# Spectral filter and expert kernel: six filter steps of the first pair exchanged by DMA, the filter in 128 rows, products of the identity ahead of stage 2

## The chip, the cores and the metric

The kernel runs on one core of a Trainium2 chip. The metric is the device time of one execution in microseconds. Three runs of the kernel before gave 2653.4, 2653.47 and 2656.06, median 2653.47. One execution was profiled.

## What is computed

Three layers follow each other on 24,576 rows of 256 float32 values (8 sequences of 3,072):

```python
def _attn_ref(x, filt_r, filt_i):             # x: (8, 3072, 256)
    X = np.fft.rfft(x, axis=1)
    return np.fft.irfft(X * (filt_r + 1j * filt_i)[None], n=x.shape[1], axis=1)

def _moe_ref(x, w_in, w_out, g_ln):           # dense layer, 1024 wide
    h = x @ w_in
    solu = h * softmax(h)
    return (layernorm(solu) * g_ln) @ w_out

def _moe2_ref(x, expert_emb, tau, w1, w2):    # 8 experts, each row goes to one
    e = argmax(normalized(x) @ normalized(expert_emb).T / tau)
    return gate * (np.maximum(x @ w1[e], 0.0) @ w2[e])
```

## The kernel before

**Filter layer.** Two sequences make a complex pair, so there are four pairs, 0 to 3. A transform of 3,072 points is split into 64 by 48. For each pair `fft` runs three stages. Stage 1 (`stage1`, 12 chunks) makes transforms of 64 on TensorE and writes them to bufA in DRAM. Stages 2 and 3 run in one loop over 16 steps j of four columns each: load the step's rows from bufA (`load2`, two DMAs in the first pair, L577), multiply with the 48-point transform (stage 2, L657), apply the filter on VectorE (`filt`), multiply with the inverse 48-point transform (stage 3, L688 to L694), evict (L695) and write to bufC in DRAM (L701). In an iteration j of the loop stand the filter of step j-1, stage 2 of step j and stage 3 of step j-2. A last transform of 64 is made in `inv4`, together with the dense layer.

The filter needs a row and its mirrored row (real with imaginary part). The first pair has it in one way, the others in another. In the first pair stage 2 stays in PSUM (tile h, two buffers, freed by the last filter product), VectorE makes two products from it (L599 with the imaginary, L600 with the real part of the filter, in zw), and stage 3 takes both with two matrices, one of them with the mirroring in it: L688 and L694. In the other pairs stage 2 is evicted by ScalarE to z in SBUF, two DMAs on SP exchange its halves of 48 rows (L669, L670, `zw<-z`), VectorE makes three products (L603, L609, L611) and stage 3 has one. These pairs run beside the dense layer; the first pair runs alone, beside the preparation of the weights (`prep_b`), of which one unit is put out after each yield of `fft`.

The filter's values for two steps (ft, 96 rows, 10 KB a row) are loaded by `load_f` on SP into one of two buffers. In the first pair load_f(0) stands behind load2(0) and load2(1).

A float32 product is two records on TensorE; a step's stage 2 is two products of 512 columns (four records), its stage 3 in the first pair four products (eight records). Each queue and each engine works in the order in which its instructions are written; SP's loads therefore wait behind an earlier load that cannot be issued yet. DMAs issued by SP and ScalarE count on one of eight semaphores, and a DMA whose semaphore is still in use waits at issue.

**Dense layer** (`stage_b`): 192 tiles of 128 rows. For a tile j the matrix product with w_out (L994) ends in a PSUM tile o; ScalarE squares it (L1002), VectorE copies eight routing columns (raw, L1019), and one iteration later `half` scales the row to two float16 parts (ScalarE L1024, VectorE L1025) and a DMA writes them to xs. After the last tile `early` is drained (tables and loads of the first expert blocks).

**Expert layer** (`stage_c`): for each block of 256 rows of one expert VectorE copies its weights (L1215, two parts), TensorE makes the first product (L1259), then the second (L1226). It starts with `weights(0, 0)`, then `next(side)`, which resumes `stage_b` at its end, then `weights(0, 1)`.

Of the kernel before, what the change touches and what calls it, by code (L numbers as in the profile page):

```python
# [24 lines left out]
E = 8  # L25
# [12 lines left out]
SPLIT = 38  # L38
WAIT = 4
SPARE = 2  # L40
TURNED = ((34, 42), (28, 42), (24, 46))
MAGIC = 0x5F3759DF

# [48 lines left out]
def layout(inputs):  # L92
    k = np.arange(KF)[None, :] + N1 * np.arange(N2)[:, None]
    k = np.minimum(k, S - k)
    f = np.stack([inputs["filt_r"][k], inputs["filt_i"][k]], axis=2)
    f = np.stack([f, f], axis=0).reshape(2 * N2, KF, 2, D)
    d = {
        "x": inputs["x"],
        "filt": f,
        "w_in": inputs["moe_w_in"],  # L100
        "w_out": inputs["moe_w_out"],
        "g_ln": np.asarray(inputs["moe_g_ln"]).reshape(8, 128).T,
        "emb": inputs["moe2_expert_emb"],
        "tau": np.asarray(inputs["moe2_tau"], dtype=np.float32).reshape(1, 1),
        "w1": inputs["moe2_w1"],
        "w2": inputs["moe2_w2"],
    }
    for n in ("w_in", "w_out"):
        if d[n].dtype == np.float64:
            d[n] = np.ascontiguousarray(d[n]).view(np.int64)  # L110
    d.update(constants())
    return {n: np.ascontiguousarray(a) for n, a in d.items()}
# [40 lines left out]
class Build:  # L153
# [390 lines left out]
    def fft(self, p, ap, ps, hp):  # L544
# [12 lines left out]
        av = bufA.rearrange("c n k d -> (c n) k d") if p else bufA.rearrange("c k n d -> c n k d")  # L557
        ld, fts, halves, zs, ys = {}, {}, {}, {}, {}

        def first(j):  # L560

            return j // 2 * KC + j % 2 * (N1 // 2)

        def load_f(j):
            if j % 2 == 0 and j < n:
                ft = ap.tile([96, KC + 1, 2, D], F32, name="ft", tag="ft")
                nc.sync.dma_start(ft, a["filt"][:, first(j):first(j) + KC + 1, :, :])
                fts[j // 2] = ft

# [22 lines left out]
        def filt(j):  # L592

            m = j % 2
            z, zw, y = zs.pop(j)
            ft = fts[j // 2]
            fr, fi = ft[:, m:m + KC, 0, :], ft[:, m:m + KC, 1, :]
            if p == 0:
                nc.vector.tensor_tensor(y, z, fi, op=ALU.mult)  # L599
                nc.vector.tensor_tensor(zw, z, fr, op=ALU.mult)  # L600
                ys[j] = (y, zw)
                return
            nc.vector.tensor_tensor(y, z, fr, op=ALU.mult)  # L603
            yield
            k = 0
            if j == 0:
                nc.vector.scalar_tensor_tensor(zw[:, 0:1, :], zw[:, 0:1, :], self.sg0, fi[:, 0:1, :], op0=ALU.mult, op1=ALU.mult)
                k = 1
            nc.vector.scalar_tensor_tensor(zw[:, k:, :], zw[:, k:, :], self.sg[m], fi[:, k:, :], op0=ALU.mult, op1=ALU.mult)  # L609
            yield  # L610
            nc.vector.tensor_tensor(y, y, zw, op=ALU.add)  # L611
            ys[j] = (y,)

        if p > 0:
            load_f(0)
            yield
            self.flush()
            yield
            yield
        load2(0)  # L620
        load2(1)
        if p > 0:
            yield
            load2(2)
            yield
            yield
            split(0)
            load2(3)
            yield
            yield  # L630
            split(1)
        else:
            load_f(0)
            load2(2)
            load_f(2)
            split(0)
        for j in range(n + 2):
            steps = filt(j - 1) if 1 <= j <= n else iter(())
            next(steps, 0)
            if j < n:  # L640
# [3 lines left out]
                a2 = halves.pop(j)  # L644
                if p == 0:
                    w = hp.tile([128, KC, D], F32, name="h", tag="h")
                    z = w[:96]
                else:
                    z = ap.tile([96, KC, D], F32, name="z", tag="z", bufs=2)
                for i in range(0, KC, b):  # L650
# [4 lines left out]
                        nc.scalar.activation(z[:, i:i + b, :], t[:96], AF.Copy)  # L655
                    else:
                        nc.tensor.matmul(w[:96, i:i + b, :], self.d2f[m], a2[:, i:i + b, :])  # L657
                    if i == 0:
                        self.flush()
                        load2(j + (4 if p > 0 else 3))  # L660
# [4 lines left out]
                    yield  # L665
                    next(steps, 0)
                zw = ap.tile([96, KC, D], F32, name="zw", tag="zw")
                if p > 0:
                    nc.sync.dma_start(zw[0:48], z[48:96])  # L669
                    nc.sync.dma_start(zw[48:96], z[0:48])  # L670
                y = ap.tile([96, KC, D], F32, name="y", tag="y", bufs=3)
# [10 lines left out]
            if j >= 2:  # L682
# [2 lines left out]
                co = ap.tile([128, KC, D], F32, name="out", tag="out", bufs=3)[:96]  # L685
                for i in range(0, KC, b):
                    t = ps.tile([128, b, D], F32, name="a", tag="a")
                    nc.tensor.matmul(t[:96], self.d3[m], y[-1][:, i:i + b, :], start=True, stop=p > 0)  # L688
                    if p == 0:
                        k = 0  # L690
                        if i == 0 and j == 2:
                            nc.tensor.matmul(t[:96, 0, :], self.d3s[0], y[0][:, 0, :], start=False, stop=False)
# [203 lines left out]
    def stage_b(self, xp, bps, gp, ps, hp, op, aux, early):  # L896
# [76 lines left out]
        for i in range(n + LAG):  # L973
# [7 lines left out]
                nc.scalar.activation(L["s"], L["h"], AF.Exp, bias=L["nm"], scale=self.isc_h[:, i // N2:i // N2 + 1], accum_out=col(i, "st", 0))  # L981
            if now:
                nc.vector.scalar_tensor_tensor(L["s"], L["h"], col(i, "cc", 0), L["s"], op0=ALU.mult, op1=ALU.mult, accum_out=col(i, "st", 1))  # L983
            if half:
                half()
                half = None
            self.catch_up()
            if 0 <= j < n:
                T = live.pop(j)["T"]
# [26 lines left out]
            if puts:  # L1016
                puts.pop()()
            if 0 <= j < n:
                nc.vector.tensor_copy(g["raw"][:, k, :], o[:, D:D + E])  # L1019
                finals = [(f, next(f) if x == 3 else x) for f, x in finals]  # L1020

                def half(j=j, k=k, o=o, c2=c2, rows=rows):
# [18 lines left out]
        for _ in early:  # L1041
            pass
        yield
        if half:
            half()
            puts.pop()()
        while finals:
            yield
            finals = [(f, x) for f, x in ((f, over(f, next(f, 1))) for f, _ in finals) if x != 1]
# [379 lines left out]
```

## Time and profile before

| | us |
|---|---|
| median of three runs | 2653.47 |
| profiled execution, whole | 2659.22 |
| its span, first to last instruction | 2657.40 |
| stage 1 of the first pair | 0 to 48.6 |
| stages 2 and 3 of the first pair | 52 to 162 |
| dense layer with the other pairs | 162 to 1600 |
| expert layer | 1603 to 2657 |

In the span TensorE is busy 2586.2 us (97%), VectorE 1864.6 (70%), ScalarE 1511.8 (57%), GpSimd 1390.7 (52%). Names in the rows: PE is TensorE's products, PEld its weight loads, DVE VectorE, ACT ScalarE, POOL GpSimd, SP SyncE; a q behind a name is that engine's queue, where DMAs are issued. Each row names the line of the kernel. PEclk is TensorE's granted clock as a share of 2.4 GHz: 0.50 is 1.2 GHz.

### The profile page before, as it was taken

Reading aid. Unit: us, or ns where it says so; the run is one execution under the profiler, and the core shown is the slowest. Engines: PE = TensorE matmul, PEld = TensorE weight load, DVE = VectorE, ACT = ScalarE, POOL = GpSimd, SP = SyncE. Lnnn points to the kernel's source line nnn. Section 1 sums busy time; section 2 is a strip of 40 time slices with the busy share of each in tenths; the row PEclk is TensorE's granted clock in tenths of the full one; section 3 lists DMA queues with packets and bytes.
Section 4 is the critical chain, followed back from the end, with each engine's and each line's share of the span. In section 5 each row is a group of like instructions: output and inputs, shape, how many; then the busy total and the mean of one; then the engine's idle time right before and its main releaser. Section 6 shows DMA issues by size and latency. Waiting matters only on the chain.

```text
span 2657.4 us, 53169 instructions
## 1 busy us (share of the span) xinstructions
PE 2586.2 (97%) x19720; PEld 1974.9 (74%) x19720; DVE 1864.6 (70%) x2955; ACT 1511.8 (57%) x2836; POOL 1390.7 (52%) x2631
## 2 busy tenths in 40 slices
PE   5989999999999999999999999999999999999998
PEld 3447666676666776666777768888888888888897
DVE  1846999869999679998899875555545545445465
ACT  2357888777888777888788862323333333333332
POOL 1001456545677445676645657655555555555444
PEclk8999999999999999999999999999999999999999
DMA  9989989999999999998655533322332222332222
GB/s 311 234 264 241 225 205 198 238 251 203 207 216 210 278 217 201 191 215 164 133 130 129 109 75 77 82 75 76 77 76 76 77 75 77 76 76 76 75 58 56
DMA packets 494997, 400.62 MB, mean 151 GB/s; under 512 B 347435, under 2 KB 417205, under 8 KB 491664
## 3 DMA queue, kind: packets, MB, share of 16 engines
q1 hardware_dynamic: 460272, 331.53, 55.3%
q0 software_dynamic: 26704, 56.16, 7.2%
q10 hardware_dynamic: 7760, 9.51, 1.2%
q8 instruction: 156, 2.56, 0.4%
q14 instruction: 105, 0.86, 0.1%
HBM read 196.46 MB, written 103.09 MB: 113 GB/s over the span
## 4 chain that ended last, share of the span: by engine, by line
PE 44%; POOL 21%; issue 20%; DVE 8%; DMA 4%; ACT 2%; POOLq 0%; SPq 0%; ACTq 0%; DVEq 0%
PE h L765 14%; PE o L994 14%; POOL crow L1181 9%; POOL out_dram L165 7%; POOL scr L164 3%; PE a L688 3%; PE h L942 3%; PE a L747 2%; PE a L514 2%; PE a L654 1%; DVE nm L931 1%; DVE es L983 1%; DMA in<-in_x_dram 1%; DVE hl L960 1%; PE o L1226 1%
## 5 line engine op out<-in xcount | busy, mean ns | idle before, releaser
L994 PE MATMUL o<-wo_h,T 128*128 128x264 f16 x3072 | 549.8, 276 | 0.3 <-issue 0.2
L1226 PE MATMUL o<-cw,chh 128*128 128x256 f16 x3152 | 522.2, 273 | 0.4 <-issue 0.4
L994 PEld LDWEIGHTS <-T 128*128 128x128 f16 x4608 | 449.9, 98 | 90.1 <-issue 22.9
L1259 PEld LDWEIGHTS <-cw 128*128 128x128 f16 x5184 | 471.2, 98 | 56.2 <-issue 6.5
L765 PE MATMUL h<-win_h,xh 128*128 128x512 f16 x1536 | 491.2, 381 | 1.8 <-ACT xh L752 0.8
L934 POOL TENSOR_SCALAR gcc<-nm 128x1 f32<-128x1 f32 x192 | 164.4, 856 | 527.2 <-DVE nm L932 527.0
L1263 DVE SCALAR_TENSOR_TENSOR chl<-h,chh 128x512 f16<-128x512 f32 x197 | 134.5, 683 | 433.1 <-ACT chh L1262 405.6
L1226 PE MATMUL o<-cw,chl 128*128 128x256 f16 x1576 | 429.6, 273 | 0.0
L765 PEld LDWEIGHTS <-xh 128*128 128x128 f16 x2304 | 221.6, 98 | 278.7 <-issue 45.9
L994 PE MATMUL o<-wo_l,T 128*128 128x264 f16 x1536 | 423.8, 276 | 0.0
L165 POOL DMA_INDIRECT out_dram<-cot,ids x197 | 213.4, 1083 | 394.4 <-ACT cot L1229 384.7
L1226 PEld LDWEIGHTS <-chh 128*128 128x128 f16 x3152 | 307.5, 98 | 35.6 <-issue 0.2
L1229 ACT ACTIVATE cot<-o,fac 128x256 f32<-128x256 f32 x197 | 93.2, 474 | 411.2 <-PE o L1226 403.5
L1215 DVE COPY cw<-wexp 128x4096 f16 x216 | 289.4, 1347 | 38.3 <-PE o L1226 25.6
L931 DVE TENSOR_REDUCE nm<-h 128x1 f32<-128x1024 f32 x192 | 234.2, 1220 | 115.1 <-PE h L765 113.5
L1259 PE MATMUL h<-cxT,cw 128*128 128x256 f16 (+1 forms) x2592 | 291.9, 264 | 4.5 <-DVE cw L1215 4.1
L1259 PE MATMUL a<-cxT,cw 128*128 128x256 f16 (+1 forms) x2592 | 291.5, 263 | 1.6 <-issue 0.8
L765 PE MATMUL h<-win_l,xh 128*128 128x512 f16 x768 | 292.1, 380 | 0.0
L1181 POOL DMA_INDIRECT crow<-xs,ids x197 | 247.5, 1256 | 63.1 <-issue 63.1
L983 DVE SCALAR_TENSOR_TENSOR es<-h,gcc,es 128x1024 f32<-128x1024 f32 x192 | 243.9, 1270 | 18.8 <-ACT es L981 8.6
L981 ACT ACTIVATE es<-h,nm,isc_h 128x1024 f32<-128x1024 f32 x192 | 230.5, 1201 | 40.0 <-DVE nm L932 39.5
L165 POOL DMA_INDIRECT lst<-gdi,gix x192 | 208.9, 1088 | 36.5 <-issue 34.3
(255 smaller groups left out, 4272.1 us busy)
## 6 DMA issues: line engine op xcount, KB each, us to landing
wst<-in_w_dram SPq DMA_DIRECT2D x128, 256.0 KB
ft<-in_filt_dram SPq DMA_DIRECT2D x32, 960.0 KB
in<-in_x_dram SPq DMA_DIRECT2D x48, 512.0 KB
c<-bufC SPq DMA_DIRECT2D x96, 256.0 KB
xs<-rows SPq DMA_DIRECT2D x96, 256.0 KB
bufA<-out SPq DMA_DIRECT2D x72, 256.0 KB
in<-bufA SPq DMA_DIRECT2D x48, 384.0 KB
zw<-z SPq DMA_DIRECT2D x96, 192.0 KB
```

Source lines behind the costliest of these rows:

```text
L165: ins = self.nc.gpsimd.indirect_dma_start(in_offset=None, **kw).ins
L765: nc.tensor.matmul(h[:, nb, :], l[:, i, db, :], r[:, db, sl], start=k == 0, stop=k == 5)
L931: nc.vector.tensor_reduce(x[:, 0:1], L["h"], axis=AX.X, op=ALU.max, negate=True)
L934: nc.gpsimd.tensor_scalar(cc, nm, nm, 1.0, op0=ALU.mult, op1=ALU.max)
L981: nc.scalar.activation(L["s"], L["h"], AF.Exp, bias=L["nm"], scale=self.isc_h[:, i // N2:i // N2 + 1], accum_out=col(i, "st", 0))
L983: nc.vector.scalar_tensor_tensor(L["s"], L["h"], col(i, "cc", 0), L["s"], op0=ALU.mult, op1=ALU.mult, accum_out=col(i, "st", 1))
L994: nc.tensor.matmul(o[:, :D + E], T[:, l, :], r[:, f, :], start=q == 0, stop=q == 23)
L1181: nc.gpsimd.indirect_dma_start(out=rows[:, h, :], out_offset=None, in_=self.xs, in_offset=bass.IndirectOffsetOnAxis(ap=tab["ids"][:, h, k: ...
L1215: nc.vector.tensor_copy(w.rearrange("p (o k) -> p o k", o=1), self.wexp[:, bass.ds(e, 1), part * 4096:(part + 1) * 4096])
L1226: nc.tensor.matmul(o[:, :D], l[f // fs][:, f % fs, h * 128:(h + 1) * 128], w2[:, r, f, :], start=q == 0, stop=q == 23)
L1259: nc.tensor.matmul(t[:, i, :], w1[:, l, db, f * 128:(f + 1) * 128], xT[:, r + db, :n], start=q == 0, stop=q == 5)
L1263: nc.vector.scalar_tensor_tensor(hl[-1][:, sl, :], t, 0.0, hh[-1][:, sl, :], op0=ALU.max, op1=ALU.subtract)
```

## The change

- `SWAPPED` names six odd steps (3 to 13) of the first pair that go the way of the other pairs: ScalarE evicts stage 2 to z (two copies, z has two buffers), SP exchanges the halves with two DMAs, VectorE makes three products, stage 3 has one product a half instead of two. `twice(j)` tells whether a step has two products.
- The filter array has 128 rows instead of 96 (zeros below), in all four pairs; VectorE reads the first 96.
- load_f(0) of the first pair stands ahead of everything else behind stage 1. Behind it stand 18 products of the 128 x 128 identity with itself into a PSUM tile that nobody reads.
- At the end of `stage_b` half of tile 190, raw of tile 191 and half of tile 191 are written behind `early` and the first yield, so in the program behind `weights(0, 0)` of the expert layer.

```diff
--- before.py
+++ after.py
@@ -38,6 +38,8 @@
 SPLIT = 38
 WAIT = 4
 SPARE = 2
+WARM = 18
+SWAPPED = (3, 5, 7, 9, 11, 13)
 TURNED = ((34, 42), (28, 42), (24, 46))
 MAGIC = 0x5F3759DF
 
@@ -94,6 +96,7 @@
     k = np.minimum(k, S - k)
     f = np.stack([inputs["filt_r"][k], inputs["filt_i"][k]], axis=2)
     f = np.stack([f, f], axis=0).reshape(2 * N2, KF, 2, D)
+    f = np.concatenate([f, np.zeros((128 - 2 * N2, KF, 2, D), f.dtype)])
     d = {
         "x": inputs["x"],
         "filt": f,
@@ -557,13 +560,17 @@
         av = bufA.rearrange("c n k d -> (c n) k d") if p else bufA.rearrange("c k n d -> c n k d")
         ld, fts, halves, zs, ys = {}, {}, {}, {}, {}
 
+        def twice(j):
+
+            return p == 0 and j not in SWAPPED
+
         def first(j):
 
             return j // 2 * KC + j % 2 * (N1 // 2)
 
         def load_f(j):
             if j % 2 == 0 and j < n:
-                ft = ap.tile([96, KC + 1, 2, D], F32, name="ft", tag="ft")
+                ft = ap.tile([128, KC + 1, 2, D], F32, name="ft", tag="ft")
                 nc.sync.dma_start(ft, a["filt"][:, first(j):first(j) + KC + 1, :, :])
                 fts[j // 2] = ft
 
@@ -594,8 +601,8 @@
             m = j % 2
             z, zw, y = zs.pop(j)
             ft = fts[j // 2]
-            fr, fi = ft[:, m:m + KC, 0, :], ft[:, m:m + KC, 1, :]
-            if p == 0:
+            fr, fi = ft[:96, m:m + KC, 0, :], ft[:96, m:m + KC, 1, :]
+            if twice(j):
                 nc.vector.tensor_tensor(y, z, fi, op=ALU.mult)
                 nc.vector.tensor_tensor(zw, z, fr, op=ALU.mult)
                 ys[j] = (y, zw)
@@ -611,8 +618,12 @@
             nc.vector.tensor_tensor(y, y, zw, op=ALU.add)
             ys[j] = (y,)
 
+        load_f(0)
+        if p == 0:
+            t = ps.tile([128, 512], F32, name="a", tag="a")
+            for _ in range(WARM):
+                nc.tensor.matmul(t[:, :128], self.ident, self.ident)
         if p > 0:
-            load_f(0)
             yield
             self.flush()
             yield
@@ -630,7 +641,6 @@
             yield
             split(1)
         else:
-            load_f(0)
             load2(2)
             load_f(2)
             split(0)
@@ -644,7 +654,7 @@
                 a2 = halves.pop(j)
                 if p == 0:
                     w = hp.tile([128, KC, D], F32, name="h", tag="h")
-                    z = w[:96]
+                    z = w[:96] if twice(j) else ap.tile([96, KC, D], F32, name="z", tag="z", bufs=2)
                 else:
                     z = ap.tile([96, KC, D], F32, name="z", tag="z", bufs=2)
                 for i in range(0, KC, b):
@@ -655,6 +665,8 @@
                         nc.scalar.activation(z[:, i:i + b, :], t[:96], AF.Copy)
                     else:
                         nc.tensor.matmul(w[:96, i:i + b, :], self.d2f[m], a2[:, i:i + b, :])
+                        if not twice(j):
+                            nc.scalar.activation(z[:, i:i + b, :], w[:96, i:i + b, :], AF.Copy)
                     if i == 0:
                         self.flush()
                         load2(j + (4 if p > 0 else 3))
@@ -665,7 +677,7 @@
                     yield
                     next(steps, 0)
                 zw = ap.tile([96, KC, D], F32, name="zw", tag="zw")
-                if p > 0:
+                if not twice(j):
                     nc.sync.dma_start(zw[0:48], z[48:96])
                     nc.sync.dma_start(zw[48:96], z[0:48])
                 y = ap.tile([96, KC, D], F32, name="y", tag="y", bufs=3)
@@ -685,8 +697,8 @@
                 co = ap.tile([128, KC, D], F32, name="out", tag="out", bufs=3)[:96]
                 for i in range(0, KC, b):
                     t = ps.tile([128, b, D], F32, name="a", tag="a")
-                    nc.tensor.matmul(t[:96], self.d3[m], y[-1][:, i:i + b, :], start=True, stop=p > 0)
-                    if p == 0:
+                    nc.tensor.matmul(t[:96], self.d3[m], y[-1][:, i:i + b, :], start=True, stop=not twice(j - 2))
+                    if twice(j - 2):
                         k = 0
                         if i == 0 and j == 2:
                             nc.tensor.matmul(t[:96, 0, :], self.d3s[0], y[0][:, 0, :], start=False, stop=False)
@@ -981,9 +993,10 @@
                 nc.scalar.activation(L["s"], L["h"], AF.Exp, bias=L["nm"], scale=self.isc_h[:, i // N2:i // N2 + 1], accum_out=col(i, "st", 0))
             if now:
                 nc.vector.scalar_tensor_tensor(L["s"], L["h"], col(i, "cc", 0), L["s"], op0=ALU.mult, op1=ALU.mult, accum_out=col(i, "st", 1))
-            if half:
+            if half and j < n - 1:
                 half()
                 half = None
+            tail, half = [half], None
             self.catch_up()
             if 0 <= j < n:
                 T = live.pop(j)["T"]
@@ -1016,7 +1029,9 @@
             if puts:
                 puts.pop()()
             if 0 <= j < n:
-                nc.vector.tensor_copy(g["raw"][:, k, :], o[:, D:D + E])
+                raw = lambda g=g, k=k, o=o: nc.vector.tensor_copy(g["raw"][:, k, :], o[:, D:D + E])
+                if j < n - 1:
+                    raw()
                 finals = [(f, next(f) if x == 3 else x) for f, x in finals]
 
                 def half(j=j, k=k, o=o, c2=c2, rows=rows):
@@ -1041,9 +1056,9 @@
         for _ in early:
             pass
         yield
-        if half:
-            half()
-            puts.pop()()
+        for f in (tail[0], raw, half):
+            f()
+        puts.pop()()
         while finals:
             yield
             finals = [(f, x) for f, x in ((f, over(f, next(f, 1))) for f, _ in finals) if x != 1]
```

## Rows read from the trace of the kernel before

**Rows 1.** Windows: busy us of each engine (instructions), PEclk, DMA share, GB/s.

```profile
20.00:30.00 10.00, 5.74 (x24) 4.31 (x24) 0.00 (x0) 2.99 (x5) 1.50 (x3) 1.00 1.03 415
...
60.00:70.00 10.00, 8.89 (x23) 5.13 (x22) 4.10 (x5) 0.78 (x2) 0.00 (x0) 0.50 1.04 186
...
65.86:148.97 83.11, 81.06 (x228) 35.56 (x227) 71.01 (x109) 35.83 (x67) 0.00 (x0) 0.95 0.98 247
```
**Rows 2.** Timeline, stage 2's start: start, us, engine, line, operation [idle before <-releaser].

```profile
47.61 1.03 PE L514 MATMUL a<-in,wst 128*128 128x256 f32 x4
...
52.34 2.10 SPq L577 DMA_DIRECT2D in<-bufA  x4
54.49 0.43 SPq L567 DMA_DIRECT2D ft<-in_filt_dram  x1
...
56.74 3.70 PE L657 MATMUL h<-in,cst 96*96 96x512 f32 x4 [8.10 <-issue]
...
65.86 1.22 DVE L599 TENSOR_TENSOR y<-h,ft 96x1024 f32<-96x1024 f32 x1 [15.88 <-DMA ft<-in_filt_dram]
67.00 1.21 DVE L600 TENSOR_TENSOR zw<-h,ft 96x1024 f32<-96x1024 f32 x1
...
68.32 3.70 PE L657 MATMUL h<-in,cst 96*96 96x512 f32 x4 [1.11 <-DVE zw L600]
```
**Rows 3.** Timeline: y of steps 2, 14, 15; last eviction of stage 3.

```profile
74.95 1.21 DVE L599 TENSOR_TENSOR y<-h,ft 96x1024 f32<-96x1024 f32 x1
...
148.97 1.21 DVE L599 TENSOR_TENSOR y<-h,ft 96x1024 f32<-96x1024 f32 x1
...
152.57 1.22 DVE L599 TENSOR_TENSOR y<-h,ft 96x1024 f32<-96x1024 f32 x1
...
161.95 0.59 ACT L695 ACTIVATE out<-a 96x512 f32<-96x512 f32 x1 [0.33 <-PE a L694]
```
**Rows 4.** Chain that ended last, in order: start us, us, what, records.

```profile
149.90 1.72 PE h L657 x4
151.62 0.86 PE a L688 x2
...
207.35 0.89 PE a L747 x8
```
**Rows 5.** Lines L609, L611, pairs 1 to 3: ns min/median/max, first, last start.

```profile
L609 DVE SCALAR_TENSOR_TENSOR zw<-zw,cst,ft x48: 1007/1274/1282, 281.9 to 1219.2; 96x1024 f32<-96x1024 f32 x45, 96x768 f32<-96x768 f32 x3
L611 DVE TENSOR_TENSOR y<-y,zw x48: 1205/1214/1240, 286.9 to 1220.6; 96x1024 f32<-96x1024 f32 x48
```
**Rows 6.** Waits of VectorE, 65 to 149 us: us in total, times, longest.

```profile
DVE es L294 <- DMA T<-in_w_in_dram: 5.0, 1, 5.0
DVE wo_l L408 <- ACT wo_h L405: 3.4, 2, 2.0
```
**Rows 7.** Waits of SP's queue, 65 to 149 us.

```profile
SPq L577 <- DMA bufC<-out: 25.4, 5, 7.7
```
**Rows 8.** Timeline: first products of TensorE after two gaps.

```profile
28.19 1.97 PE L514 MATMUL a<-in,wst 128*128 128x256 f32 x8 [3.24 <-DMA wst<-in_m_dram]
...
192.42 2.07 PE L514 MATMUL a<-in,mt 128*128 128x256 f32 x4 [3.83 <-ACT out L515]
```
**Rows 9.** Timeline where the expert stage begins.

```profile
1600.54 0.17 DVE L1019 COPY graw<-o 128x8 f32<-128x8 f32 x1 [4.70 <-ACT rows L1002]
...
1601.91 1.47 DVE L1215 COPY cw<-wexp 128x4096 f16 x1
...
1603.49 2.55 PE L1259 MATMUL h<-cxT,cw 128*128 128x256 f16 x12 [4.05 <-DVE cw L1215]
...
1605.83 2.11 PE L1259 MATMUL a<-cxT,cw 128*128 128x256 f16 x12
...
1607.77 1.47 PE L1259 MATMUL h<-cxT,cw 128*128 128x256 f16 x12
```
**Rows 10.** Windows, columns as in rows 1: 100 us under the other pairs.

```profile
500.00:600.00 100.00, 99.30 (x669) 74.25 (x668) 67.02 (x129) 70.66 (x135) 41.96 (x123) 1.00 1.01 259
```

## The prediction

> **What bounds the kernel now.** I read the windows first, to see which engine is full in the stages that the diff touches, then the timeline where stage 2 of the first pair starts, then who waits for whom there, and last the timeline where the expert stage begins. Between these two places TensorE is busy 99% of a typical 100 us [rows 10], so a microsecond won in either should arrive whole at the end.
>
> Stage 1 ends at 47.61 + 1.03 = 48.6 us. Its rows go out to DRAM and come back, and the first product of stage 2 starts at 56.74, at half speed: four records span 3.70 us, where they later take 1.72 [rows 2, 4]. The clock stays at 0.50 from 60 to 70 [rows 1]. VectorE cannot start its first filter product until 65.86: it stood 15.88 us, and what came last was the filter, ft, queued on SP behind four loads that need stage 1's rows [rows 2]. From that product to the one of step 14 (65.86 to 148.97, 83.11 us) TensorE is busy 81.06 us, VectorE 71.01, and the DMA engines 0.98 of the time, at 247 GB/s [rows 1, 3]. One engine is full, but two others stand close behind it, and that decides what the swap is worth.
>
> **The change, part by part.** The sum is made against the profiled span of 2657.40 (2659.22 with what lies around it). The median of the three runs is 2653.47, 5.75 lower; I take the same differences off it.
>
> *Start of stage 2.* load_f(0) no longer stands behind loads that wait for bufA and can issue while SP idles before 52.34 [rows 2]. The 15.88 us wait goes, and step 0's product is late next. The 18 products are 36 records of 128 columns. Eight such take 0.89 us [rows 4], so 36 take 4.0: from 48.6 to 52.6. They lie in idle time and cost nothing unless the first load lands before that, and at 52.34 it is only being issued. They leave a gap of 52.6 to 56.7, 4.1 us. The nearest rows: after 3.24 us of idle, eight records of 256 columns still took 1.97 us, but after 3.83 us four took 2.07 [rows 8]. The gap is nearer to the second, so I take half speed for the start of stage 2, and full speed as the other bound. At half speed TensorE goes as in the trace up to h(2), which there waited 1.11 us for zw(0) [rows 2]; without that it starts at 67.2 and ends 3.70 later, so y(2) starts at 70.9 against 74.95 [rows 3]: **4.0 us won**. At full speed VectorE's own chain decides, with its first product at 56.74 + 1.72 = 58.5: 7.3 us.
>
> *Six exchanged steps.* On TensorE each loses the L688 product in both halves, two times 0.86 us [rows 4], 10.3 us in all. But VectorE gets three products from SBUF instead of two from PSUM, two of 1.21 us and one of 1.27 [rows 5]; two follow each other 1.14 apart (65.86 and 67.00), so a step costs about 1.25 more, 7.5 in all. ScalarE gets two copies a step of 0.59 us each, like an eviction of the same size [rows 3], 7 us in all, under 47 us of idle (busy 35.83 of 83.11 [rows 1]); without that cover each would make the exchange 0.6 us later. So from y(0) to y(14) VectorE's work goes from 71.0 to 78.5, and TensorE's falls to about 68.5 (81.1, less 8.6 for five swapped steps whose stage 3 lies inside, less 4 for the part at half speed). VectorE becomes the engine that paces. Its idle in the stretch, 12.1 us now, then counts in full: 5.0 for one T load, 3.4 for ScalarE, the rest in small waits [rows 1, 6]. ScalarE's stay. The T loads have no ft(0) in front of them any more and should come earlier by about as much as VectorE does. I take 7.5 us of idle, with bounds of 4 and 12. The stretch becomes 78.5 + 7.5 = 86.0 instead of 83.1: **2.9 lost**. After y(14) TensorE had a backlog: 13.0 us to the last eviction at 161.95. With VectorE pacing there is none: 3.6 us to y(15), 2.35 for its two products and four times 0.86 on TensorE, 9.4 in all [rows 3, 4]: **3.6 won**.
>
> The new wait is VectorE's on the exchange. Its second product of a swapped step blocks all that stands behind it in order: the preparation's conversions, the next filter product, and through that TensorE's h of a later step. SP issues the two DMAs behind in(j+3) and ft, and behind any wait of these; SP already spends 25.4 us there on bufC stores before it can issue a load [rows 7]. A step's rows are ready some 8 us after VectorE finished step j-3 (h, four products, h, a copy) and wanted 13 to 19 us after it, so 5 to 11 us are free for the transfer. I count nothing beyond the 7.5; the bad bound is the third rival.
>
> *Filter in 128 rows.* By bytes each of the 32 loads grows by a third. With loads of 128 rows the engines moved 415 GB/s at a share of 1.03, with loads of 96 and 48 rows 186 at 1.04 [rows 1]. So the price of one lies between 1.31 MB at 247 GB/s, 5.3 us, and at 415, 3.2, against 4.0 for 0.98 MB now. I take the middle, nothing. The 24 of the other pairs lie under a TensorE that idles 0.7 us in 100 [rows 10]: nothing, with 3 us either way. The Trainium skill (SBUF — State Buffer, Door 1: The DMA port swizzle) says that rows 0 to 63 reach only eight of sixteen ports. By that the upper 32 rows use ports that 96 rows leave half idle, and the larger load would take no longer than now, where by bytes alone at 247 GB/s the eight of the first pair would add 10.6 us of transfer. The rows at 415 and 186 lean to the page.
>
> *Entry of the expert stage.* Before the first weight copy (1601.91) stand half(190) and raw(191), which wait for ScalarE; raw(190) ends at 1600.71. They move behind the copy: 1.2 us. TensorE's gap of 4.05 us shrinks to 2.9, under the 3.24 that kept full speed; the first two groups start 2.34 and 1.94 us apart instead of 1.31, up to 1.7 more [rows 8, 9]. half(191), which waits for POOL, is late with or without them. **2.0 won**, bounds 1.2 and 2.9.
>
> Sum: 4.0 - 2.9 + 3.6 + 2.0 = 6.7; 2653.5 - 6.7 = **2646.8**.
>
> **Rivals.**
> *The clock holds* through the gap, so the change does at its start what its products can do at most: 7.3 for 4.0, 2643.5. For: the gap is 0.3 us over one that fell, and loads may land sooner. Against: it is over it.
> *TensorE's saving arrives.* VectorE waits for almost nothing, 4 us of idle in the stretch: 7.3 + 0.6 + 3.6 + 2.9 = 14.4, 2639; with no idle at all 2635. For: a T load without ft(0) in front. Against: ScalarE's 3.4 us, and that VectorE's 78.5 us cannot shrink.
> *The DMA engines pace.* For: a share of 0.98. y(14) stays at 148.97, and only 3.6 and 1.2 are won: 2648.7.
> *Slower: the transfers cost bytes.* The stage gains 2.36 MB of exchange and seven times 0.33 MB of filter and loses ft(0)'s 0.98. At the stage's 247 GB/s that is 18.8 - 4.0 = 14.8 us before y(14); less 3.6 and 1.2, 10 slower: 2663.5. It turns from gain to loss once y(14) comes 4.8 us later than now. For: 3.5 us for each exchange is no more than what SP's waits there cost [rows 7]. Against: of VectorE's waits in the stretch only 5.0 us are for a DMA in one place, the rest small [rows 6].
> That the products hold no clock at all, so that this part of the change does not do what it says, is the forecast.
>
> **How the numbers follow.** Forecast 0.36 (own range 2643 to 2650), clock held 0.22, saving arrives 0.10, DMA engines pace 0.18, slower 0.14 (2654 to 2663.5). The measurement can tell some 0.2%, 5.3 us, from no change; that puts the lines at 2648.2 and 2658.8. A quarter of the forecast, two thirds of the DMA case and a fifth of the slower one lie between them. Faster: 0.27 + 0.21 + 0.10 + 0.06 = 0.64; same: 0.09 + 0.01 + 0.12 + 0.03 = 0.25; slower 0.11. The range 2638 to 2656 leaves out about a tenth on either side.
>
> **What would show it.** Right: no wait of y on ft at step 0; y(2) near 71 and y(14) near 148; VectorE busy above 0.88 of the stretch between y(0) and y(14), TensorE with gaps ahead of h in even steps; the last eviction of the pair near 157; the first expert product 1.2 us nearer to the last o product. Wrong: VectorE standing for zw<-z over 3 us a step; ft landing no sooner at 128 rows; the clock still at 0.50 past 74; TensorE full between y(0) and y(14).

## The result and the profile after

| | before | after |
|---|---|---|
| median, us (four runs each) | 2654.76 | 2671.72 |
| lowest and highest | 2653.40 to 2656.88 | 2664.48 to 2677.74 |
| ratio after / before | | 1.0062, 95% interval 1.0047 to 1.0077 |
| profiled execution: whole, span | 2659.22, 2657.40 | 2664.48, 2662.70 |

The change costs 16.5 us (0.0062 of 2654.8) where I forecast a gain of 6.7. The profiled execution of after is the shortest of its four, and that of before lies above all four of its runs. So the two spans differ by only 5.3 us; what they show of the place and the mechanism holds, their difference as a size does not.

The windows of after, with the columns of [rows 1]: the 10 us at the start of stage 2, and the stretch from the filter's y(0) to y(14).

```profile
60.00:70.00 10.00, 10.00 (x26) 5.33 (x25) 4.72 (x6) 0.52 (x2) 0.00 (x0) 0.55 1.06 290
63.33:164.86 101.53, 87.42 (x224) 37.40 (x225) 78.01 (x115) 44.11 (x82) 0.00 (x0) 0.87 0.81 242
```

The stretch that took 83.11 us takes 101.53. VectorE has the work that I gave it (78.01, forecast 78.5), but is busy for 0.77 of the time, not for the 0.88 and more that I expected. TensorE, with 10.3 us of products fewer in the six steps, stands for 14 us and runs at a mean clock of 0.87 instead of 0.95. The DMA engines fall from 0.98 to 0.81. No engine is full any more: something makes them wait for each other.

The timeline of after, from the end of stage 1 to the last eviction of stage 3 (L625 the 18 products, L667 h, L310 a conversion of the weights' preparation, L606 y of a step with two products, L707 the eviction):

```profile
51.34 4.48 PE L625 MATMUL a<-cst 128*128 128x128 f32 x36
...
59.59 3.70 PE L667 MATMUL h<-in,cst 96*96 96x512 f32 x4 [3.77 <-issue]
...
63.33 1.22 DVE L606 TENSOR_TENSOR y<-h,ft 96x1024 f32<-96x1024 f32 x1 [11.43 <-PE h L667]
...
69.46 1.88 PE L667 MATMUL h<-in,cst 96*96 96x512 f32 x4
...
73.82 0.69 DVE L310 TENSOR_TENSOR pw<-es 128x512 f32<-128x512 f32 x1
...
74.43 1.21 DVE L606 TENSOR_TENSOR y<-h,ft 96x1024 f32<-96x1024 f32 x1
...
164.86 1.21 DVE L606 TENSOR_TENSOR y<-h,ft 96x1024 f32<-96x1024 f32 x1
...
175.72 0.59 ACT L707 ACTIVATE out<-a 96x512 f32<-96x512 f32 x1 [0.33 <-PE a L706]
```

Against [rows 2, 3]: the 15.88 us wait for ft is gone and y(0) comes 2.5 us earlier, y(2) still 0.5 earlier; y(14) comes 15.9 later, the last eviction 13.8. In these two executions all of the loss arises between y(2) and y(14), among the exchanged steps. Of the 13.8 us, 8.5 are not in the span: the dense layer, from that eviction to its last product, took 1430.6 us for 1436.9, since the gap of 3.83 us at its start [rows 8] with the half clock behind it did not occur in this execution (in that of e2, below, it did, with 1436.1), and the expert stage 2.3 less. Two waits of after, 70 to 160 us, are new there (waiter, its line, whom for: us in total, times, longest):

```profile
PE h L667 <- ACT z L669: 13.6, 6, 3.2
...
DVE zw L616 <- DMA zw<-z: 13.8, 3, 6.8
```

The second I had as a risk, the first not at all. One of the six waits for the copy, step 9, in the timeline of after:

```profile
122.03 1.02 PE L667 MATMUL h<-in,cst 96*96 96x512 f32 x2
122.23 0.59 ACT L707 ACTIVATE out<-a 96x512 f32<-96x512 f32 x1 [1.12 <-PE a L706]
...
122.85 1.64 ACTq L713 DMA_DIRECT2D bufC<-out  x2
...
124.54 1.06 ACT L720 ACTIVATE jk<-out 96x1024 bf16<-96x1024 f32 x1 [1.72 <-issue]
...
125.50 0.19 ACT L720 ACTIVATION_READ_ACCUMULATOR jk<-out 96x1 f32 x1
125.59 0.57 ACT L669 ACTIVATE z<-h 96x512 f32<-96x512 f32 x1
126.22 1.25 PE L667 MATMUL h<-in,cst 96*96 96x512 f32 x2 [3.17 <-ACT z L669]
```

TensorE makes the first half of h and then stands 3.17 us, until ScalarE has copied that half, although the second half goes to other columns of the tile. ScalarE comes to the copy only behind an eviction, the issue of the two stores and the square sum of an earlier step, all in the order in which they are written. That happens in all six steps. After each of five of these six gaps the records of the granted clock show a stretch at 0.50 (from 79.25, 96.32, 127.04, 140.69 and 154.35; 20.5 us in all), where before ran at 1.00 from 74.53 on, until 190.6. For step 9 the windows are, the first half of h with the gap, then the stretch that follows:

```profile
122.03:126.22 4.19, 1.02 (x3) 0.16 (x2) 4.19 (x6) 2.22 (x4) 0.00 (x0) 1.00 0.81 240
127.04:130.45 3.41, 3.41 (x5) 0.85 (x3) 3.41 (x6) 1.19 (x2) 0.00 (x0) 0.50 1.01 341
```

The second wait is seen best in the chain of waits of after at step 5 (start us, us, what):

```profile
92.68 8.84 DMA bufC<-out
101.53 0.33 SPq L584
...
102.45 0.52 SPq L681
...
103.02 5.02 DMA zw<-z
...
108.14 1.28 DVE zw L616
...
110.48 1.13 DVE y L618
...
112.86 1.21 DVE y L606
```

z is complete at 97.0, but SP is held by a load that waits for a store's semaphore (8.84 us; it is the wait of [rows 7]) and issues the exchange at 102.45. The second transfer takes 5.02 us, and y of the next step stands behind all of it on VectorE. In step 3 the exchange is late too (z complete at 81.19, issued at 85.21), but not by a load: SP's waits name stage 3's product there (L700), which reads the tile zw. VectorE stands 5.6 us in step 3 and 6.8 in step 5. In the other four steps SP issues the exchange as soon as z is complete, and VectorE stands 1.4 us in one of them and not at all in three.

### The profile page after: what moved, and what is told of

It is laid out like the page before. It is cut to its first block, busy times and chain, and to the rows that moved or that the text cites. A ratio compares the mean times of both kernels' runs of the same rounds, so it can differ in the third digit from the quotient of the medians.

```text
span 2662.7 us, 53239 instructions
## 1 busy us (share of the span) xinstructions
PE 2587.0 (97%) x19732; PEld 1977.0 (74%) x19732; DVE 1870.1 (70%) x2961; ACT 1517.5 (57%) x2848; POOL 1388.2 (52%) x2631
## 4 chain that ended last, share of the span: by engine, by line
PE 48%; POOL 21%; issue 20%; DVE 5%; DMA 3%; ACT 2%; POOLq 0%; SPq 0%; another core or an unknown queue 0%; ACTq 0%; DVEq 0%
PE h L777 16%; PE o L1007 16%; POOL crow L1196 9%; POOL out_dram L168 7%; POOL scr L167 3%; PE a L700 3%; PE a L759 3%; PE h L954 3%; PE a L517 3%; PE a L664 2%; PE h L667 1%; DMA in<-in_x_dram 1%; POOL lst L168 1%; DVE nm L943 1%; DVE es L995 1%
## 5 line engine op out<-in xcount | busy, mean ns | idle before, releaser
L946 POOL TENSOR_SCALAR gcc<-nm 128x1 f32<-128x1 f32 x192 | 158.7, 826 | 534.6 <-DVE nm L944 534.4
L995 DVE SCALAR_TENSOR_TENSOR es<-h,gcc,es 128x1024 f32<-128x1024 f32 x192 | 243.8, 1270 | 18.8 <-ACT es L993 8.0
```

The costliest lines, as they stand in the source:

```text
L946: nc.gpsimd.tensor_scalar(cc, nm, nm, 1.0, op0=ALU.mult, op1=ALU.max)
```

## The experiments

Times are ratios to the kernel before on the same chip, with 95% intervals; 0.001 is 2.65 us. "Clock loss" is (1 - mean granted clock) times the span, averaged over all runs of a kernel; that of before was 23.0, 21.6 and 21.8 us in the first three groups of runs (e1 to e4, e5 to e8, e9 to e12) and 20.6 in the fourth, that of after is 32.0.

**e1: everything but the exchanged steps.**

```diff
-SWAPPED = (3, 5, 7, 9, 11, 13)
+SWAPPED = ()
```

> All of the change but the six exchanged steps: every step of the first pair keeps its two products and has no exchange; filter in 128 rows, early ft(0), the 18 products and the later end of the dense layer stay. Theory: the whole loss sits in the exchanged steps, so this one is faster than before: about 0.5 to 4 us from the start of stage 2 and 2.3 from the entry of the expert stage, 2648 to 2652, with no half clock between 80 and 160 us. Rival (the wider filter or the start costs): it stays above before, 2658 to 2670.

Measured: 0.9989 (0.9976 to 1.0001), clock loss 19.9. The loss is gone. Of the 2.8 to 6.3 us that the rest should win, about 3 may be there, at the edge of what the interval can tell from nothing.

**e2: the exchanged steps alone**, on the kernel before (the filter in 96 rows, its start and its end of the dense layer).

```diff
+SWAPPED = (3, 5, 7, 9, 11, 13)
...
-            if p == 0:
+            if twice(j):
...
```

> The kernel before with the six exchanged steps and nothing else. Theory (loss in the exchanged steps): slower than after by what the other parts win, 3 to 6 us, so 2674 to 2680 for a median of 2671.7 of after; y(14) 15 us or more later than before. Rival (wider filter costs): near before, 2652 to 2660, since the exchange would cost nothing with a filter of 96 rows.

Measured: 1.0057 (1.0036 to 1.0078), clock loss 36.1; the profile has y(14) at 168.22. So the loss of after, 1.0062, is the exchanged steps' own, and the wider filter has no part in it. The time came out below the 2674 that I expected at least, because the rest wins less than I gave it.

**e3: the copy of h once, behind both products.**

```diff
                         nc.tensor.matmul(w[:96, i:i + b, :], self.d2f[m], a2[:, i:i + b, :])
-                        if not twice(j):
-                            nc.scalar.activation(z[:, i:i + b, :], w[:96, i:i + b, :], AF.Copy)
...
+                if p == 0 and not twice(j):
+                    nc.scalar.activation(z, w[:96], AF.Copy)
```

> After, with ScalarE's copy of h made once behind both products of an exchanged step instead of one copy behind each; everything else as in after. In after the second product of each exchanged step waits for the copy of the first half: TensorE stands 13.6 us in six places between 76 and 155 us, and five stretches at half clock, 20.5 us together, follow these gaps. Theory A (this wait is the loss): the six gaps and the half clocks go, y(14) comes 12 us or more earlier, 2648 to 2656. Theory B (the exchange's landing is the loss, VectorE stands 13.8 us for it and all else waits behind): the gaps move to another wait, 2664 to 2672.

Measured: 1.0027 (1.0015 to 1.0038), clock loss 29.3. Half of the loss goes. The wait for the copy is gone from h and partly comes back ahead of stage 3, while VectorE's wait stays (waits of e3, 70 to 160 us):

```profile
PE a L700 <- ACT z L678: 4.0, 2, 2.1
PE a L700 <- DVE y L618: 4.0, 3, 2.0
...
DVE zw L616 <- DMA zw<-z: 12.6, 4, 4.1
```

The median, 2663.6, is at the lower edge of what the second theory gave and far from the first's: the gaps have moved, as that one says, and still half of the loss is gone, which it doesn't.

**e4: no exchange.** VectorE's second operation reads z in place of the exchanged zw.

```diff
-                if not twice(j):
+                if p > 0:
                     nc.sync.dma_start(zw[0:48], z[48:96])
                     nc.sync.dma_start(zw[48:96], z[0:48])
...
-            nc.vector.scalar_tensor_tensor(zw[:, k:, :], zw[:, k:, :], self.sg[m], ...
+            nc.vector.scalar_tensor_tensor(zw[:, k:, :], (zw if p else z)[:, k:, :], self.sg[m], ...
```

> After, with the two exchange transfers of the six steps left out: VectorE's second product reads z itself, so the result of these steps is not the filter's, while all instructions on TensorE, VectorE and ScalarE stay. Theory A (TensorE's wait for the copy): only part comes back, TensorE still stands 2 us or more ahead of the second product in each of the six steps, 2660 to 2668. Theory B (landing of the exchange): VectorE's 13.8 us go and with them most of the loss, 2648 to 2656.

Measured: 1.0044 (1.0029 to 1.0059), clock loss 30.2. VectorE's 13.8 us are gone from the waits, and only 4.8 us of time come back, as the first theory has it (its 2660 to 2668 was a little low); TensorE stands nearly as in after, 1.4 to 2.4 us in each of the six steps (waits of e4, 70 to 160 us):

```profile
PE h L667 <- ACT z L669: 12.7, 6, 2.4
```

**e5: both cures**, the edits of e3 and e4 together.

> The two cures together: after, with ScalarE's copy made once behind both products, and without the exchange's transfers (VectorE reads z itself, so the filter of the six steps is not computed). Alone the first gave 8.2 us of the 16.7 that after loses, the second 3.1. Theory A (two waits in series, each standing where the other one goes): together they give back all, 2650 to 2656, and the clock stays at 1.00 from 70 to 160 us. Theory C (VectorE's third product a step paces, as the forecast had it): the two only add, 2657 to 2663, with TensorE still standing for VectorE's products.

Measured: 0.9991 (0.9982 to 1.0000), clock loss 22.1. All of the loss is given back: 18.8 us from after, against 9.3 and 4.8 for the two cures alone. The two waits lie one behind the other, and each covers part of the other's removal. In one thing the first theory did not hold: the clock isn't at 1.00 throughout, 10.2 us from 125.5 on are at 0.50.

**e6: work in the gap.** Eight products of the identity between the two halves of h in the six steps, written where the second half goes.

```diff
+                        if not twice(j) and i == 0:
+                            for _ in range(FILL):
+                                nc.tensor.matmul(w[:, b, :128], self.ident, self.ident)
                         if not twice(j):
                             nc.scalar.activation(z[:, i:i + b, :], w[:96, i:i + b, :], AF.Copy)
```

> After, with eight products of the identity (16 records of 0.11 us, 1.8 us) between the two products of each exchanged step, into the half of the same tile that the second product then overwrites: TensorE works where it stood 2.3 us, and nothing else moves. Theory (clock): the stretches at half clock between 75 and 160 us go, and with them the share of the loss that the mean granted clock shows (0.988 against 0.991 over 2660 us, some 8 us): 2662 to 2666. Rival (only the standing counts): 2670 to 2674.

Measured: 1.0033 (1.0022 to 1.0044), clock loss 20.2 instead of 32.0. Useless work in a gap makes the kernel 7.7 us faster (0.0029 of 2654, some 5 us either way), as the theory of the clock has it; on the chip of these runs before took 2651.0, so the 2659.1 measured stand for 2663 beside the others. The windows 75 to 160 us, first of after, then of e6, show the clock in the column PEclk: 0.88 and 0.96. Not all of the half clock went: 6.8 us from 121.8 on are left. The 7.7 us rest on all runs of the two kernels; in the one profiled execution of each, the time from the end of stage 1 to the pair's last eviction is the same, 124.2 us in after (its fastest run) and 124.0 in e6.

```profile
75.00:160.00 85.00, 70.89 (x174) 28.69 (x173) 64.19 (x97) 38.38 (x72) 0.00 (x0) 0.88 0.77 231
```

```profile
75.00:160.00 85.00, 78.64 (x277) 39.43 (x277) 67.27 (x100) 42.40 (x77) 0.00 (x0) 0.96 0.80 241
```

**e7: e5 without VectorE's third operation.**

```diff
-            nc.vector.tensor_tensor(y, y, zw, op=ALU.add)
+            if p > 0:
+                nc.vector.tensor_tensor(y, y, zw, op=ALU.add)
```

> The kernel of the two cures together, and in the six steps VectorE's third operation, the sum, is left out as well: two operations a step as before the change, one product less on TensorE, and nothing of the exchange (the result of these steps is not the filter's). Theory C (VectorE's third operation eats TensorE's saving): 5 to 8 us below the run with the two cures alone. Theory A: the same within 3 us, since VectorE has room.

Measured: 0.9990 (0.9981 to 0.9999), against 0.9991 with it. VectorE's longer work, on which my sum of the stretch rested, isn't what the time hangs on. The profiles show how: from y(2) to y(14) e7 takes 72.2 us and e5 76.7, but the last eviction of the pair comes 109.3 and 110.0 us after the end of stage 1.

**e8: the end of the dense layer alone**, on the kernel before (its diff is the last three hunks of the change).

> The kernel before with the later end of the dense layer alone. Forecast: 2.0 us faster, bounds 1.2 and 2.9, from the entry of the expert stage; the traces of before and after show 2.2 there. Rival (the entry is bound otherwise): no difference.

Measured: 1.0002 (0.9994 to 1.0011). There is no gain to be seen; 2.0 us (0.9992) lie outside the interval, the lower bound of 1.2 (0.9995) does not. The first products of the expert stage after the last product of the dense layer, first in e2, which has the old end, then in e8:

```profile
1617.85 1.47 PE L1267 MATMUL h<-cxT,cw 128*128 128x256 f16 x12 [2.13 <-issue]
```

```profile
1593.26 1.49 PE L1270 MATMUL h<-cxT,cw 128*128 128x256 f16 x12 [1.32 <-DVE cw L1226]
```

The gap falls from 2.13 to 1.32, and it is 1.32 in all fifteen profiles with the new end. The old end is in two profiles only: 4.05 with half clock behind it in [rows 9], and the 2.13 of e2.

**e9: work in the gap and no exchange**, the edits of e6 and e4.

> After, with the eight products of the identity between the two products of each exchanged step and without the exchange's transfers (VectorE reads z itself, so the filter of the six steps is not computed). The second product still waits for ScalarE's copy. Theory (of the loss the clock is one part and the exchange's landing the other, while TensorE's standing for the copy costs by its clock alone): 0.998 to 1.001 of before, as with the two cures together (0.9991). Rival (TensorE's standing is time on the path too): 1.003 or more, as with the filling products alone (1.0033).

Measured: 1.0020 (1.0010 to 1.0030), clock loss 19.8. Its windows 75 to 160 us have the clock at 1.00:

```profile
75.00:160.00 85.00, 80.50 (x297) 41.07 (x295) 72.20 (x106) 44.90 (x81) 0.00 (x0) 1.00 0.78 245
```

It lies between the two: the theory wanted 0.998 to 1.001, the rival 1.003. With clock and exchange out of the way, the place where TensorE waits for the copy still costs what separates this run from e5, 7.7 us; so TensorE's time there was on the path. Up to some 2 us of it may be the filling's own: in two steps ScalarE stood 0.9 and 0.4 us until the last filling product had ended, and from the first half of h to the second the six steps take 14.8 us together, where e4, without filling, takes 12.7.

So the loss of after against e5, 18.8 us, splits in this order: clock 7.7 (after to e6), exchange 3.5 (e6 to e9), TensorE's time in the gap 7.7 (e9 to e5), each known to 4 to 5 us either way, so that the 3.5 can't be told from nothing. The order matters. Taken away last, behind the copy, the exchange is worth 9.6 (e3 to e5), known to 4 either way.

**e10, e11, e12: the other parts, without exchanged steps.** e10 has the filter in 96 rows, e11 no products, e12 more products; each against e1.

```diff
-                ft = ap.tile([128, KC + 1, 2, D], F32, name="ft", tag="ft")
+                ft = ap.tile([96, KC + 1, 2, D], F32, name="ft", tag="ft")
```

```diff
-            t = ps.tile([128, 512], F32, name="a", tag="a")
-            for _ in range(WARM):
-                nc.tensor.matmul(t[:, :128], self.ident, self.ident)
+            pass
```

```diff
-WARM = 18
+WARM = 32
```

> Early ft(0), the 18 products and the later end of the dense layer, no exchanged step, and the filter in 96 rows as before the change. Forecast: the wider filter costs nothing (3 us either way for the other pairs), so this one lies within 0.1% of the run with the filter in 128 rows (0.9989 of before). Rival (bytes count): 2 to 4 us faster than that, 0.9975.

> Filter in 128 rows, early ft(0) and the later end of the dense layer, no exchanged step, and no products in front of stage 2. Forecast: the 18 products end some 3.8 us before the first product of stage 2 and hold no clock, so the time is that of the run with them (0.9989 of before). Rival (they shorten the half clock): 1 to 3 us slower, 0.9995 to 1.0000.

> No exchanged step, everything else of the change, and 32 products in front of stage 2 instead of 18: 64 records of 0.12 us fill 8 of the 8.1 us between stage 1 and the first product of stage 2. Theory (the gap of 3.8 us that the 18 leave is what lowers the clock at 58 to 68 us): the clock stays at 1.00 there, y(2) comes 2 to 4 us earlier, 0.997 to 0.998 of before. Rival (loads and VectorE set the pace there): the clock stays up and y(2) comes less than 1 us earlier, 0.9985 to 0.9995.

Measured: e10 1.0000 (0.9991 to 1.0009), e11 0.9998 (0.9988 to 1.0008), e12 0.9992 (0.9983 to 1.0000), beside 0.9989 (0.9976 to 1.0001) of e1. The four can't be told apart, nor, but for a little, from before. The rival of e10, 0.9975, lies outside its interval, so the wider filter costs nothing that these runs can tell; that of e11, 0.9995 to 1.0000, has the measured 0.9998 in it, and its interval holds the forecast of 0.9989 too, so the time doesn't decide whether the 18 products help. What the products do to the clock can be told: with 18 and with none it is at 0.50 until 68 us, with 32 it is not. The timeline and windows of e12:

```profile
56.56 1.93 PE L667 MATMUL h<-in,cst 96*96 96x512 f32 x4 [0.87 <-issue]
58.53 1.22 DVE L606 TENSOR_TENSOR y<-h,ft 96x1024 f32<-96x1024 f32 x1 [8.97 <-PE h L667]
...
67.63 1.21 DVE L606 TENSOR_TENSOR y<-h,ft 96x1024 f32<-96x1024 f32 x1
```

```profile
60.00:70.00 10.00, 10.00 (x39) 5.26 (x38) 9.73 (x14) 2.31 (x5) 0.00 (x0) 1.00 1.09 265
```

h(0) takes 1.93 us instead of 3.70, y(2) comes 19.1 us after the end of stage 1 (48.55) instead of 22.8 (e1: 73.68 - 50.93), and the clock loss falls to 14.7 from the 19.9 to 20.5 of its neighbours. Of these 4 to 6 us the ratios show 1 (0.9992 against 0.9996, the mean of the other three), with intervals of 2 to 3 us either way: the clock and y(2) came as the theory has them, the time as its rival.

**e13, e14, e15: the exchange from another queue**, on e3: from ScalarE right behind its copy, from POOL, and from POOL with 32 products.

```diff
-                    nc.sync.dma_start(zw[0:48], z[48:96])
-                    nc.sync.dma_start(zw[48:96], z[0:48])
+                    q = nc.sync if p else nc.scalar
+                    q.dma_start(zw[0:48], z[48:96])
+                    q.dma_start(zw[48:96], z[0:48])
```

(in e14 and e15 `nc.gpsimd` for `nc.scalar`.)

> After, with the copy made once behind both products, and the exchange's two transfers issued by ScalarE right behind its copy instead of by SP. With SP the copy made once gave 1.0027 of before, without any exchange 0.9991. Theory (SP's order): VectorE's wait for zw<-z, 12.6 us there, falls below 5 us and the time to 0.999 to 1.001. Rival (the transfer itself): the wait stays near 12 us, 1.002 to 1.004; ScalarE's own waits for the store's lanes may move the exchange instead.

> The same with the two transfers issued by POOL, which has nothing else to do in this stretch. Theory (SP's order): as with ScalarE's queue or better, 0.999 to 1.001. Rival (the transfer itself): 1.002 to 1.004.

> The same from POOL's queue with 32 products in front of stage 2 instead of 18. Without exchanged steps 32 products gave 0.9992 and y(2) at 67.6 us. If TensorE's saving of six products arrives once the waits are gone: 0.996 to 0.998. If it is lost to VectorE's work and to other small waits, as in the run with the two cures (0.9991): 0.999 or more.

Measured: 1.0042 (1.0028 to 1.0055), 1.0053 (1.0040 to 1.0067), 1.0039 (1.0026 to 1.0053). None is better than e3 with SP's queue. In e14 the copy itself releases POOL's issue in four of the six steps, and yet the view of the tile zw (70 to 160 us) reads:

```profile
  DMA zw<-z: 11.6, 5
...
DMA to landing us min/median/max: 2.8/7.0/8.7
```

VectorE's wait is 11.6 us in e14 and 12.6 in e13, where SP's queue gave 12.6 in e3: it stays, as the rivals have it, and the times of e13 and e14 lie even a little above the rivals' 1.002 to 1.004; e15 is with its second forecast, 0.999 or more. That doesn't clear SP's order, which held the exchange of step 5 for 5.5 us in after and for 6.6 in e3. The other queues issue it 0.3 us or less after z is complete, but their transfers land later. From its issue to the last update of its semaphore, a transfer of 192 KB took in the median of twelve 3.6 us from SP in after and 4.2 in e3, 5.1 from ScalarE (e13) and 7.3 from POOL (e14; the view above has six of the twelve). What was won at the issue was lost on the way; why the same transfer takes longer from these queues was not tried. The Trainium skill (DMA: Bandwidth & Descriptors, Issuing engines are not separate DMA queues) says that the DMAs of all issuing engines run on the same sixteen engines. The trace agrees in that another queue brought no sooner landing: from 75 to 160 us the DMA share is 0.84 in e3, 0.86 in e13 and 0.89 in e14.

No working version of the exchange came near the kernel without it (1.0027 to 1.0062 against 0.9989 to 1.0000).

## Why the prediction was wrong

*Start of stage 2, 4.0 won.* The mechanism was right: no wait on ft, and step 0's product is next. The clock, too: with 18 products it stays at 0.50, as with none (e11), because they leave a gap of 3.8 us; e12 shows that it takes products up to 0.9 us before the first of stage 2. The size was off, for two reasons. The sum let y(2) start where h(2) ends; but in before 2.9 us lay between the two (72.02 and 74.95 [rows 2, 3]) and in after 3.1 (71.34 and 74.43), in which VectorE made the preparation's conversions. And I measured from one profile. From the end of stage 1 to y(2) before took 26.3 us (74.95 - 48.64) and after 22.9; but e2 and e8, with the old start, took 23.5 and 23.8. By these two some 1 us was won, by the mean of the three 1.6, not 4.0.

*Six exchanged steps, 2.9 lost: this step failed.* VectorE's work was sized well (78.01 for 78.5), and that it would pace was wrong (e7). The term that failed is its idle in the stretch: 7.5 us in the sum, 23.5 measured (101.53 - 78.01), so that the stretch lost 18.4 us and not 2.9; TensorE, for which I had 68.5 us of work there, was busy 87.4. Two sentences carried the error. "ScalarE gets two copies a step of 0.59 us each ... under 47 us of idle": idle time in sum isn't idle time at the place. ScalarE works in order, the copy stands behind some 3 us of an earlier step's evictions and sums (step 9), and I did not ask who waits for the copy other than the exchange. The diff answers it: the copy of one half of h is written ahead of the product of the other half, in one tile. I looked at what the new instructions cost, and not at what an instruction already there now has to wait for. The Trainium skill (PSUM — Partial Sum Buffer, PSUM bank collisions raise a hardware error) wants two engines apart only within one bank, 2 KiB; each half of h, 512 float32 values, is a bank by itself, so that rule doesn't ask for this wait. The trace has it all the same, six times; why the program is ordered so was not tried.

The other sentence: "5 to 11 us are free for the transfer. I count nothing". VectorE stood 13.8 us. The reckoning took "ready some 8 us after" from TensorE's and ScalarE's work alone, without the gap. And the risk that stood beside it, that SP issues the exchange behind waits of its own, came true in step 5: the exchange was issued 5.5 us after z was complete, and VectorE stood 6.8. In step 3 it was issued 4.0 us after, behind a reader of zw that the reckoning did not have, and VectorE stood 5.6. The transfers themselves took 2.9 to 5.8 us in after, 3.6 in the median.

And no term of the sum had the clock of this stretch in it. I had weighed it at the start of stage 2, from [rows 8], and took it for settled past 74.5; yet the forecast itself wanted TensorE to have gaps ahead of h. Gaps of 1.5 to 3.2 us cost 7.7 us by the clock (e6) and about as much again by the time in them (e9 to e5), both with the margins given there.

*Behind y(14), 3.6 won.* The backlog fell from 13.0 to 10.9 us (175.72 - 164.86), 2.1. The reason given, VectorE's longer work, fits the profiles of e5 and e7: with its third operation 10.0 us lie between y(14) and the last eviction, without it 14.0.

*Filter in 128 rows, nothing.* Right: e10 and e1 can't be told apart. The six later loads of the first pair landed after 8.2 us on average in e1 and 8.0 in e11, with 128 rows, and after 8.3 in e10 and 7.8 in before, with 96, though the bytes grow by a third. The Trainium skill's port rule (SBUF — State Buffer, Door 1: The DMA port swizzle) would have it so, and the trace agrees.

*Entry of the expert stage, 2.0 won.* Not to be seen (e8). The gap shrank as forecast, but the row of before that I took it from, 4.05 with the half clock behind it, had 2.13 in e2. By these rows it is worth 0.8.

*The rivals.* "Slower: the transfers cost bytes" has the sign, and its 2663.5 is nearer than anything else I wrote. The exchange is a part: 3.5 us of the loss, 9.6 if the copy is cured first (e3 to e5). The larger loads, half of its price, cost nothing that can be told (e10), and bytes did not pace the stage, whose DMA share fell from 0.98 to 0.81. "TensorE's saving arrives" falls even without both waits: e5 has 10.3 us of TensorE's products less than e1 and, within 4 us, the same time (0.9991, 0.9989). Where these 10.3 us go was not settled. From 70 to 160 us the profile of e5 has TensorE standing 6.9 us in six places for ScalarE and VectorE, where that of e1 has none, and 10.2 us at half clock, which cost 5.1: together about as much as was saved.

*What would have shown it.* Of the signs that I named as wrong, VectorE standing for zw<-z over 3 us a step is there in two of the six steps. "The clock still at 0.50 past 74" is there in another form: not still, but again.

## What to carry to other kernels

Where a change puts a read of another engine between two writes into one tile, ask whether the second write now waits for it, and for how long that engine is busy at this place, in its own order; its idle share says nothing of that. Here work taken off an engine that was full opened gaps, and on TensorE five of the six were paid twice, by themselves and by the clock behind them, so count the clock wherever a forecast says "stands". And take no saving from one row of one execution: look for the same gap in another profile first.

## What the runs showed of the hardware

- Six gaps of TensorE of 1.5 to 3.2 us within 80 us, in a stretch where it was busy 87.4 of 101.5 us, were followed in five places by a fall of the granted clock to 0.50, 20.5 us in all (after). Filling them with eight useless products brought the clock loss from 32.0 to 20.2 us and the time down by 7.7, some 5 either way (e6).
- A gap of 0.87 us in front of stage 2 kept 1.00 (e12), one of 3.8 us did not (after, e1).
- Transfers of 192 KB from SBUF to SBUF took 2.9 to 5.8 us from SP's queue in after (median 3.6) and 2.9 to 8.6 in e3 (4.2), 2.9 to 6.8 from ScalarE's (e13, 5.1) and 2.8 to 8.7 from POOL's (e14, 7.3), in a stage where the DMA engines are busy 0.77 (after) to 0.89 (e14) of the time.
- The end of stage 1 lies between 48.5 and 52.3 us in the profiles of all these kernels, though each engine has the same instructions in the first 40 us.
